# Sums of w_out from three pairs of buffers, four of the seven blocks by way of DRAM; weight blocks, x pieces and the first steps in another order

## The chip, the cores and the metric

One core of a Trainium2 chip runs the whole program. The metric is the device time of one execution in microseconds (us), the median of the runs shown. The engines are PE (TensorE, matrix products), DVE (VectorE), ACT (ScalarE), POOL (GpSimd) and SP (SyncE, which here issues the DMAs, in program order).

## The reference, cut to what matters

```python
def _attn_ref(q, k, v, g_norm):                  # q, k, v: 8 x 8 heads x 576 x 64
    kv = np.einsum('bhsd,bhse->bhde', k, v)
    out = np.einsum('bhsd,bhde->bhse', q, kv)
    rms = np.sqrt(np.mean(out * out, axis=-1, keepdims=True) + 1e-06)
    return (out / rms * g_norm).astype(np.float32)

def _moe_ref(x, w_in, w_out):                    # x: 4608 x 512, w_in: 512 x 2048, w_out: 2048 x 512
    h = x @ w_in
    g = h * np.cos(h)
    return (g @ w_out).astype(np.float32)

def _moe2_ref(x, w1, w2, w3, w_out):             # 512 -> 1024 -> 1024 -> 512
    h = (x @ w1) * (x @ w2) @ w3
    return (h @ w_out).astype(np.float32)

# reference: the attention's output as 4608 x 512 goes through _moe_ref, its result through _moe2_ref
```

## The kernel before, in words

**Three stages.** The attention and the product h = x @ w_in run together, in 144 steps; then g @ w_out in 63 parts; then the second MLP. A float32 operand of a product is split into a high and a low half (`split`: ACT copies the high half, DVE or POOL subtracts it for the low half), and a product is three passes of matmuls (`three`, L863 to L865).

**The steps.** Step n takes one block of 512 tokens and one of 16 column blocks of w_in: 12 matmuls of 128x512 into one of four PSUM banks (`emit_h`, emitted one step ahead). ACT takes the whole turns from h (r, L1392), DVE subtracts them (u, L1393), ACT takes the sine (L1366), and one step later DVE multiplies by h (u, L1367), which frees the bank: h of step n+4 waits for that product of step n. After each pair of column blocks POOL makes four differences of g (`form`, L828 to L831: tiles ta and tb), and SP stores u, ta and tb to DRAM tensors g, the seven right blocks of a seven-product scheme. Beside this run, placed by step numbers in `phases`: the attention of the later units of tokens (`plan_unit`: its squares, Newton steps for the norms on DVE, scaling `o` on POOL, L359), the pieces of x (`split_x`, high half ACT, low half DVE, L124), and the conversion of weight words to float32 (`plan_words`, `plan_w_in`: one ACT and four DVE operations per block, L152 to L160; w_out's blocks go to DRAM, tensors w_out). `first_steps` writes steps 0 to 7 by hand: its list `begins` says when a w_in block's conversion starts, `norms` computes the first units' norms on DVE, `rows` spreads them with matmuls on PE (L462), `scale` applies them, `split_x(1, c)` prepares the second x block.

**The left blocks.** From w_out, for each of four row pairs kk, come seven left blocks wl_l_kk: l = 0 and 1 are halves as they are, l = 2 is a half too, l = 3, 4, 5, 6 are sums and differences made one after the other in place. `left_load(kk)` loads the four pieces of w_out (256 KB each) into one pair of buffers of the `g` tag. `left_plain(kk)` (steps 124 to 136) splits l = 0 and 1. For the sums the pair is loaded again: kk = 0 at step 137 (`left_sums` at steps 139 to 141), kk = 1 at step 142, kk = 2 and 3 after the parts 1 and 3, with `left_sums` in parts 0 to 5 (lines L933 to L940 are its additions, on DVE, for kk = 2 and 3 two of four on POOL).

**The parts.** NS is 144; "NS+i" in the code is part i. Part i is 24 matmuls (L995) of a right block g_hl_i (1 MB, loaded by `load_right` four parts ahead as g_raw, split by `split_right` two parts ahead: ACT high, DVE or POOL low) with the left blocks l of its product, kk = 0 and 1 in the first half and 2 and 3 in the second. The order of products takes l = 0, 1, 4, 3, 5, 2, 6, two parts each; so the parts 0 to 3 need l = 0 and 1, the parts 4 and 5 l = 4, the parts 6 to 13 l = 3, 5, 2 and 6.

**What sets the order.** Through both stages the order of each engine's instructions is the program's, written out by hand; each engine, and SP's queue of DMAs, takes its instructions in that order, and an instruction that waits holds all behind it on its engine.

## Time and profile before

| what | value |
|---|---|
| median of the runs shown (3) | 1515.92 us (1515.26 to 1516.95) |
| the profiled execution | 1524.87 us, its span 1523.1 us |
| PE busy | 1462.8 us (96%) |
| DVE, ACT, POOL busy | 1011.2, 695.6, 598.7 us |
| mean granted clock of PE | 0.984 |
| moved by DMA | 295.60 MB, mean 194 GB/s |

The steps run from about 45 us to 553 us of the span, the parts from 553 us to about 910 us, and the second MLP after that. Busy times are unions of the instructions' times; PE's matmuls overlap in the records, so what a stretch of PE is worth is read from the number of its matmuls, not from its busy share. The clock column gives the share of full speed that PE was granted in a stretch.

### The profile page before, as it was taken

To read this page: it belongs to the slowest core of one execution; us is meant where nothing else is said; L and a number is where in the kernel's file an instruction comes from. 1 tells how busy PE (TensorE), PEld (TensorE's weight loads), DVE (VectorE), ACT (ScalarE), POOL (GpSimd) and SP (SyncE) were. 2 spreads that over 40 slices of the span, in tenths; PEclk is the share of its full clock that TensorE was granted. 3 is DMA by queue.
4 is the path that set the end of the run, shared out by engine and by line. 5 is a ranking of instruction groups with operands and counts; after the bars stand their busy time and mean duration, and the time that the engine had idled before them with its cause. 6 is when DMAs were issued, how large, how long until landed. Compare 5 with 4: busy or idle time off the path is not lost.

```text
span 1523.1 us, 21182 instructions
## 1 busy us (share of the span) xinstructions
PE 1462.8 (96%) x7632; PEld 1248.5 (82%) x7632; DVE 1011.2 (66%) x1489; ACT 695.6 (46%) x1320; POOL 598.7 (39%) x423
## 2 busy tenths in 40 slices
PE   8999999899989985999999998999999999999998
PEld 6777777676767864898888887999999988999997
DVE  3888876687686785899999337755544546545543
ACT  4556555445544544555555435434433334333331
POOL 0043862644464552212121326455444237344330
PEclk9999999999999997999999999999999999999999
DMA  8256986867765975999999765122102313233312
GB/s 317 98 181 216 304 255 187 281 206 262 246 223 185 353 262 189 338 356 358 365 365 352 254 206 180 42 77 76 70 29 83 112 62 110 75 101 124 125 63 77
DMA packets 143529, 295.60 MB, mean 194 GB/s; under 512 B 16096, under 2 KB 49984, under 8 KB 143424
## 3 DMA queue, kind: packets, MB, share of 16 engines
q1 hardware_dynamic: 142720, 293.66, 56.4%
q8 instruction: 60, 0.98, 0.3%
q10 hardware_dynamic: 704, 0.59, 0.1%
q14 instruction: 45, 0.37, 0.1%
HBM read 184.92 MB, written 109.27 MB: 193 GB/s over the span
## 4 chain that ended last, share of the span: by engine, by line
PE 80%; DVE 9%; DMA 4%; issue 3%; POOL 2%; ACT 1%; SPq 1%; ACTq 0%; POOLq 0%; DVEq 0%
PE X L1213 13%; PE X L995 12%; PE V L995 6%; PE V L1213 6%; PE h L863 6%; PE h L864 6%; PE h L865 6%; PE o L864 4%; PE o L863 4%; PE o L865 4%; PE Y L1213 3%; PE Y L995 3%; PE kv L272 2%; DVE x L124 2%; DVE u L1393 1%
## 5 line engine op out<-in xcount | busy, mean ns | idle before, releaser
L863 PE MATMUL h<-x,w_in 128*128 128x512 f32 x576 | 238.7, 414 | 11.8 <-DVE u L1367 11.8
L1213 PE MATMUL X<-xc,w 128*128 128x384 f32 x1152 | 226.2, 337 | 5.3 <-DVE wchl L124 3.1
L864 PE MATMUL h<-x,w_in 128*128 128x512 f32 x576 | 227.8, 395 | 1.6 <-DVE x L124 1.6
L865 PE MATMUL h<-x,w_in 128*128 128x512 f32 x576 | 227.1, 394 | 0.0
L124 POOL TENSOR_TENSOR xc<-x2r,xc 128x768 fp32r<-128x768 f32 x70 | 134.8, 1936 | 228.5 <-ACT xc L122 228.5
L995 PE MATMUL X<-g_hl,wl 128*128 128x512 f32 (+1 forms) x960 | 204.0, 372 | 17.9 <-ACT wl L122 13.3
L1213 PEld LDWEIGHTS X<-xc,w 128*128 128x128 f32 x1152 | 203.9, 188 | 13.0 <-DVE wchl L124 3.5
L995 PEld LDWEIGHTS X<-g_hl,wl 128*128 128x128 f32 x960 | 169.4, 191 | 49.9 <-ACT wl L122 14.1
L122 ACT ACTIVATE g_hl<-g_raw 128x1024 fp32r<-128x1024 f32 x126 | 126.3, 1051 | 101.3 <-PE V L995 34.9
L124 POOL TENSOR_TENSOR g_hl<-g_raw,g_hl 128x1024 fp32r<-128x1024 f32 x31 | 79.1, 2553 | 226.6 <-ACT g_hl L122 202.7
L1393 DVE SCALAR_TENSOR_TENSOR u<-h,r 128x512 f32<-128x512 f32 x136 | 93.3, 686 | 93.5 <-ACT r L1392 80.9
L863 PEld LDWEIGHTS h<-x,w_in 128*128 128x128 f32 x576 | 109.7, 190 | 44.6 <-DVE u L1367 15.6
L124 DVE TENSOR_TENSOR g_hl<-g_raw,g_hl 128x1024 fp32r<-128x1024 f32 x95 | 114.0, 1228 | 48.0 <-ACT g_hl L122 47.9
L1392 ACT ACTIVATE r<-h 128x512 int32<-128x512 f32 x136 | 81.0, 596 | 139.4 <-PE h L865 138.9
L1221 ACT ACTIVATE s<-X 128x384 f32<-128x384 f32 x144 | 66.7, 488 | 152.7 <-PE X L1213 152.6
L864 PEld LDWEIGHTS h<-x,w_in 128*128 128x128 f32 x576 | 109.9, 191 | 26.1 <-DVE x L124 4.0
L865 PEld LDWEIGHTS h<-x,w_in 128*128 128x128 f32 x576 | 109.6, 190 | 23.6
L1213 PE MATMUL V<-xc,w 128*128 128x384 f32 x576 | 116.2, 335 | 0.0
L863 PE MATMUL o<-wchl,ab 128*128 128x512 f32 x288 | 112.3, 391 | 0.7 <-DVE part L1304 0.6
L864 PE MATMUL o<-wchl,ab 128*128 128x512 f32 x288 | 113.0, 392 | 0.0
L865 PE MATMUL o<-wchl,ab 128*128 128x512 f32 x288 | 110.5, 393 | 0.0
L1366 ACT ACTIVATE u<-u 128x512 f32<-128x512 f32 x136 | 85.1, 626 | 51.3 <-DVE u L1393 51.3
(175 smaller groups left out, 2590.4 us busy)
## 6 DMA issues: line engine op xcount, KB each, us to landing
g_raw<-g SPq DMA_DIRECT2D x126, 512.0 KB
x2r<-x_all SPq DMA_DIRECT2D x44, 384.0 KB
kvraw<-in_kv_main_dram SPq DMA_DIRECT2D x32, 512.0 KB
g<-ta SPq DMA_DIRECT2D x32, 512.0 KB
g<-tb SPq DMA_DIRECT2D x32, 512.0 KB
g<-u SPq DMA_DIRECT2D x28, 512.0 KB
g<-u SPq DMA_DIRECT2D x40, 256.0 KB
part<-o SPq DMA_DIRECT2D x36, 256.0 KB
```

What stands on the lines that cost most here:

```text
L122: hi = nc.scalar.activation(dst[:, 0], src, AF.Copy)
L124: lo = lo_engine.tensor_tensor(dst[:, 1], src, f32(dst[:, 0]), ALU.subtract)
L272: nc.tensor.matmul(ps[d], k[:, d], v[:, d], start=fresh and i == 0, stop=i == NC, skip_group_check=True,)
L863: nc.tensor.matmul(ps, w[0], x[0], start=first, stop=False)
L864: nc.tensor.matmul(ps, w[0], x[1], start=False, stop=False)
L865: return nc.tensor.matmul(ps, w[1], x[0], start=False, stop=last).ins
L995: nc.tensor.matmul(ps, w[:, a, i2, ws], g[:, b, q], start=first and half == 0 and q == 0 and n == 0, stop=last and final and q == KH - 1 a ...
L1213: nc.tensor.matmul(ps, w[:, self.i, a, k], x[:, b, k], start=first and k == 0 and n == 0, stop=last and k == 1 and n == 2, skip_group_chec ...
L1221: copied.append(nc.scalar.activation(s, ps, AF.Copy).ins)
L1366: nc.scalar.activation(u, u, AF.Sin, bias=HALF_PI, scale=TWO_PI)
L1392: nc.scalar.activation(r, h_ps[n], AF.Identity, bias=0.25, scale=INV_2PI)
L1393: nc.vector.scalar_tensor_tensor(u, h_ps[n], INV_2PI, r, ALU.mult, ALU.subtract)
```

## The change

Five things change.

1. **First steps.** The conversion of the fourth w_in block of this stage starts at step 6 instead of step 3. `emit_h(6)` moves ahead of `rows(0)` and goes to the bank acc3; `emit_h(7)` moves ahead of `rows(2)`. `scale` and `split_x(1, c)` follow in another order.
2. **Units and weight words.** The last three units of the attention start at steps 78, 86, 93 instead of 77, 84, 91; eight of sixteen w_out blocks are converted at other steps.
3. **x pieces.** How many pieces go into a step is counted by their width, and in five ranges of steps (`LIGHT`) their low half is made on POOL instead of DVE.
4. **w_out's left blocks.** `left_load` uses three pairs of buffers (g0 and g1, wc0 and wc1, wc2 and wc3, and g0 and g1 again), each loaded once, at steps 117, 120, 121 and 127. `left_stage(kk, 0..3)` makes the sums at the steps 122+4kk to 125+4kk and splits l = 0, 1 and 4 at once; some additions go to POOL. `left_store` writes the sums for l = 3, 5 and 6 to DRAM (12 stores of 256 KB); l = 2 is read again from w_out. In the parts 0 to 7 `left_late` splits the four late blocks, two row pairs at a time, from a tile w_pair (512 KB) that `left_pair` loads two parts ahead.
5. **Loads ahead.** The first four `load_right` go to the steps 131, 135, 138 and 140 (before 126, 130, 134, 142), the first `split_right` to 138 (before 133); the conversion of the second MLP's weights starts in part 9 (before 8), its loads in part 7 (before 6).

```diff
@@ -582,7 +582,7 @@
         group = [begin()]
         emit_h(0)
         emit_h(1)
-        begins = (1, 1, 1, 1, 0, 0, 0, 0)
+        begins = (1, 1, 1, 0, 0, 0, 1, 0)
         for n in range(HM):
             attends = n < NPAIR
             new = []
@@ -590,8 +590,10 @@
                 rows(1)
             if n == 6:
                 rows(3)
-            if 1 <= n < HM - 1:
+            if 1 <= n < HM - 3:
                 emit_h(n + 1)
+            if n == 4:
+                emit_h(6, "acc3")
...
                 norms(sums, x, y, t)
                 rows(0)
             if n == 5:
+                emit_h(7)
                 scale(0)
                 rows(2)
+                split_x(1, 0)
             if n == 6:
                 scale(2)
-                split_x(1, 1)
-            if n == 7:
                 split_x(1, 2)
+                scale(3)
+                split_x(1, 3)
...
             if n == 5:
                 scale(1)
-                split_x(1, 0)
-            if n == 6:
-                scale(3)
+                split_x(1, 1)
...
-        split_x(1, 3)
         emit_h(HM)
 
     plan = {}
@@ -844,7 +845,7 @@
         at(n + lag, "top", store, 2, ta, tag_a)
         at(n + lag + (lag > 2), "top", store, 4, tb, tag_b)
 
-    def split_x(t, c, units=None):
+    def split_x(t, c, units=None, lows=None):
         if t not in x_hl:
             x_hl[t] = x_home(t % 3, [P, 2, KD, TB], F32R, f"x_{t}")
         done = 0
@@ -854,7 +855,7 @@
             if units is None or u in units:
                 made = split(
                     x_hl[t][:, :, c, done:done + w], o_sb[u][:, c, s:s + w],
-                    None if t == 0 else nc.vector,
+                    None if t == 0 else lows or nc.vector,
                 )
...
-    def emit_h(n):
+    def emit_h(n, tag=None):
         t, m = steps[n]
-        if n <= HM or n % 4 < 2:
+        if tag:
+            ps = ps_acc.tile([P, 512], F32, tag=tag, name=f"h_{n}")
+        elif n <= HM or n % 4 < 2:
             ps = ps_h.tile([P, 512], F32, tag="h", name=f"h_{n}")
         else:
             ps = ps_acc.tile([P, 512], F32, tag=f"acc{n % 4 - 2}", name=f"h_{n}")
@@ -892,19 +895,29 @@
 
     w_left = {}
 
-    def left_raw(kk, which):
-        t = g_home([P, 2, DM], F32, f"w_out_{which}{kk}")
-        for i in range(2):
-            nc.sync.dma_start(out=t[:, i], in_=later["w_out", 4 * kk + 2 * i + which])
-        return t
+    LEFT_TAGS = (("g0", "g1"), ("wc0", "wc1"), ("wc2", "wc3"), ("g0", "g1"))
+    sums_d = {}
+    lefts = {}
+
+    def left_load(kk):
+        f = []
+        for which, tag in enumerate(LEFT_TAGS[kk]):
+            name = f"w_out_{which}{kk}"
+            if tag[0] == "g":
+                t = g_home([P, 2, DM], F32, name, tag)
+            else:
+                t = homes["p2"].tile([P, 2, DM], F32, tag=tag, name=name)
+            for i in range(2):
+                nc.sync.dma_start(out=t[:, i], in_=later["w_out", 4 * kk + 2 * i + which])
+            f.append(t)
+        lefts[kk] = f
 
     def left_home(l, kk):
         if l == 0:
             return homes["p2"], f"wc{4 + kk}"
-        if l == 1:
-            return wpool, f"wi{kk}"
-        at = 4 + 5 * kk + (4, 3, 5, 2, 6).index(l)
-        return wpool, f"wi{at}" if at < NM else f"u{at - NM}"
+        if l in (2, 6):
+            return wpool, f"u{4 * (l == 6) + kk}"
+        return wpool, f"wi{4 * (1, 4, 3, 5).index(l) + kk}"
 
     def left(l, kk, src):
         pl, tag = left_home(l, kk)
@@ -912,34 +925,53 @@
         split(t, src, vec)
         w_left[l, kk] = t
 
-    lefts = {}
-
-    def left_load(kk):
-        lefts["at"] = left_raw(kk, 0), left_raw(kk, 1)
-
-    def left_plain(kk):
-        h = slice(0, DM // 2)
-        f0, f1 = lefts.pop("at")
-        left(0, kk, f0[:, :, h])
-        left(1, kk, f1[:, :, h])
-
-    def left_sums(kk, stage):
-        f0, f1 = lefts["at"]
+    def left_stage(kk, stage):
+        f0, f1 = lefts[kk]
         h = DM // 2
         a11, a21, a12, a22 = f0[:, :, 0:h], f0[:, :, h:], f1[:, :, 0:h], f1[:, :, h:]
-        adder = vec if kk < 2 else pool
         if stage == 0:
-            left(2, kk, a22)
-            vec.tensor_tensor(a22, a21, a22, ADD)
-            left(3, kk, a22)
+            (vec if kk < 2 else pool).tensor_tensor(a22, a21, a22, ADD)
+            left(0, kk, a11)
         if stage == 1:
-            adder.tensor_tensor(a21, a11, a21, SUB)
-            vec.tensor_tensor(a22, a22, a11, SUB)
-            left(4, kk, a22)
+            (pool if kk else vec).tensor_tensor(a21, a11, a21, SUB)
+            left(1, kk, a12)
         if stage == 2:
-            adder.tensor_tensor(a12, a12, a22, SUB)
-            left(5, kk, a21)
-            left(6, kk, a12)
+            vec.tensor_tensor(a11, a22, a11, SUB)
+        if stage == 3:
+            (pool if kk else vec).tensor_tensor(a12, a12, a11, SUB)
+            left(4, kk, a11)
+
+    def left_store(kk, l):
+        if l not in sums_d:
+            sums_d[l] = dram.tile([P, 4, 2, DM // 2], F32, name=f"w_left_{l}")
+        f0, f1 = lefts[kk]
+        h = DM // 2
+        src = {3: f1[:, :, h:], 5: f0[:, :, h:], 6: f1[:, :, 0:h]}[l]
+        nc.sync.dma_start(out=sums_d[l][:, kk], in_=src)
+
+    LATE_LEFT = [(l, q) for l in (3, 5, 2, 6) for q in range(2)]
+    pairs_l = {}
+
+    def left_pair(i):
+        if i >= len(LATE_LEFT):
+            return
+        l, q = LATE_LEFT[i]
+        t = g_home([P, 2, 2, DM // 2], F32, f"w_pair_{l}{q}")
+        if l == 2:
+            for k in range(2):
+                for e in range(2):
+                    c = 4 * (2 * q + k) + 2 * e + 1
+                    nc.sync.dma_start(out=t[:, k, e], in_=later["w_out", c][:, DM // 2:])
+        else:
+            nc.sync.dma_start(out=t, in_=sums_d[l][:, 2 * q:2 * q + 2])
+        pairs_l[i] = t
+
+    def left_late(i):
+        l, q = LATE_LEFT[i]
+        t = pairs_l.pop(i)
+        for k in range(2):
+            left(l, 2 * q + k, t[:, k])
+        left_pair(i + 2)
 
 
     parts_of = []
@@ -1313,9 +1345,10 @@
         }
         end_of = {t: max(n for n, s in enumerate(steps) if s[0] == t) for t in range(NB)}
         ready = plan_first(HM - 1)
-        starts = (14, 22, 29, 36, 44, 52, 59, 77, 84, 91)
+        starts = (14, 22, 29, 36, 44, 52, 59, 78, 86, 93)
         for u, n in zip(range(6, NU), starts):
             ready[u] = plan_unit(u, n, u in (6, 9, 10, 11, 12, 13))
+        LIGHT = (*range(48, 54), *range(64, 72), *range(80, 88), *range(98, 104), *range(114, 120))
         pieces = []
         for u in range(NHALF + 1, NU):
             for t in range(2, NB):
@@ -1324,37 +1357,37 @@
                     pieces.append((t, max(ready.get(u, 0), free) + 1, u))
         taken_up = {}
         for t, n, u in sorted(pieces):
+            w = min((t + 1) * TB, (u + 1) * HALF) - max(t * TB, u * HALF)
+            most = {4: 4, 5: 2}.get(u, 2 if t in (2, 3, 6) or u == 14 else 1.3) * HALF
             for c in range(KD):
-                while taken_up.get(n, 0) >= (4 if u == 4 else 2):
+                while taken_up.get(n, 0) + w > most:
                     n += 1
-                taken_up[n] = taken_up.get(n, 0) + 1
-                assert n < begin_of[t] - 1
-                at(n, "pieces", split_x, t, c, (u,))
+                taken_up[n] = taken_up.get(n, 0) + w
+                assert n < begin_of[t] - 1, (t, n, u, c)
+                at(n, "pieces", split_x, t, c, (u,), pool if n in LIGHT else vec)
         i = state["conv"]
         for k in range(i, n_first):
-            plan_w_in(k, (8, 9, 10, 12, 14, 16, 18, 20)[k - i])
-        words = (22, 36, 39, 52, 54, 67, 70, 73, 76, 79, 92, 95, 98, 101, 104, 107)
+            plan_w_in(k, (8, 9, 10, 12, 14, 16, 18)[k - i])
+        words = (22, 37, 39, 52, 54, 67, 69, 73, 75, 81, 93, 95, 99, 101, 105, 107)
         for k, n in enumerate(words):
             plan_words(n_first + k, n)
         for kk in range(4):
-            at(121 + 4 * kk, "top", left_load, kk)
-            at(124 + 4 * kk, "mid", left_plain, kk)
-        at(126, "end", load_right, 0)
-        at(130, "end", load_right, 1)
-        at(133, "mid", split_right, 0)
-        at(134, "end", load_right, 2)
-        at(137, "top", left_load, 0)
-        for k in range(3):
-            at(139 + k, "mid", left_sums, 0, k)
+            n = 122 + 4 * kk
+            at((117, 120, 121, 127)[kk], "end", left_load, kk)
+            for k in range(4):
+                at(n + k, "mid", left_stage, kk, k)
+            for l, k in ((3, 2), (5, 3), (6, 5)):
+                at(n + k, "top", left_store, kk, l)
+        at(131, "end", load_right, 0)
+        at(135, "end", load_right, 1)
+        at(138, "mid", split_right, 0)
+        at(138, "end", load_right, 2)
         at(140, "mid", split_right, 1)
-        at(142, "top", left_load, 1)
-        at(142, "end", load_right, 3)
-        for kk, n in ((1, 0), (2, 2), (3, 4)):
-            at(NS + n, "mid", left_sums, kk, 0)
-            at(NS + n, "mid", left_sums, kk, 1)
-            at(NS + n + 1, "mid", left_sums, kk, 2)
-            if kk < 3:
-                at(NS + n + 1, "end", left_load, kk + 1)
+        at(140, "end", load_right, 3)
+        at(NS - 2, "end", left_pair, 0)
+        at(NS - 1, "end", left_pair, 1)
+        for i in range(len(LATE_LEFT)):
+            at(NS + i, "mid", left_late, i)
 
         def do(n, where):
             for f in plan.pop((n, where), ()):
@@ -1413,10 +1446,10 @@
                 load_right(i + 4)
             if state["conv"] > state["put"]:
                 put(1)
-            if 8 <= i and state["conv"] < state["load"]:
+            if 9 <= i and state["conv"] < state["load"]:
                 convert(1)
-            if 6 <= i:
-                prefetch(min(state["conv"] + 2, len(chunks)))
+            if 7 <= i:
+                prefetch(min(state["conv"] + (1 if i == 7 else 2), len(chunks)))
             part(i)
             do(NS + i, "mid")
             do(NS + i, "end")
```

The order of instructions in three places; in the names, the last number counts tiles.

PE, first steps, before: h_5 ends, the first norms' rows (spread) follow, then h_6.

```order
L864 MATMUL h_5_673<-x_0_421,w_in_5_582 128x512
L865 MATMUL h_5_673<-x_0_421,w_in_5_582 128x512
L865 MATMUL h_5_673<-x_0_421,w_in5_582 128x512
L462 MATMUL spread_2_0_700<-rs_first_97 64x96 x6
L462 MATMUL spread_3_0_707<-rs_first_97 64x96 x6
L462 MATMUL spread_2_1_723<-rs_first_97 64x96 x6
L462 MATMUL spread_3_1_730<-rs_first_97 64x96 x6
L863 MATMUL h_6_737<-x_0_421,w_in6_627 128x512
```

PE at the same place, after.

```order
L866 MATMUL h_5_671<-x_0_421,w_in5_582 128x512
L864 MATMUL h_6_684<-x_0_421,w_in6_627 128x512
...
L866 MATMUL h_6_684<-x_0_421,w_in6_627 128x512
L462 MATMUL spread_2_0_711<-rs_first_97 64x96 x6
L462 MATMUL spread_3_0_718<-rs_first_97 64x96 x6
L462 MATMUL spread_2_1_727<-rs_first_97 64x96 x6
L462 MATMUL spread_3_1_734<-rs_first_97 64x96 x6
L864 MATMUL h_7_744<-x_0_421,w_in7_666 128x512
```

h_6 stands between h_5 and the first rows now; h_7 likewise stands ahead of the third row set.

DVE, parts 2 and 3, before: wl is a low half of a left block, w_out a sum in place, g_hl a low half of a right block.

```order
L124 TENSOR_TENSOR g_hl_4_5441<-g_raw_4_0_5345,g_hl_4_5441 128x1024
L124 TENSOR_TENSOR g_hl_4_5441<-g_raw_4_1_5347,g_hl_4_5441 128x1024
L124 TENSOR_TENSOR wl_2_2_5476<-w_out_12_5436,wl_2_2_5476 128x512
L933 TENSOR_TENSOR w_out_12_5436<-w_out_02_5433,w_out_12_5436 128x2x256
L124 TENSOR_TENSOR wl_3_2_5480<-w_out_12_5436,wl_3_2_5480 128x512
L937 TENSOR_TENSOR w_out_12_5436<-w_out_12_5436,w_out_02_5433 128x2x256
L124 TENSOR_TENSOR wl_4_2_5485<-w_out_12_5436,wl_4_2_5485 128x512
L124 TENSOR_TENSOR g_hl_5_5488<-g_raw_5_0_5394,g_hl_5_5488 128x1024
```

DVE at the same place, after: w_pair is the tile loaded from the stored sums, s1 a sum of results (it stood a few rows lower before).

```order
L124 TENSOR_TENSOR g_hl_4_5448<-g_raw_4_0_5361,g_hl_4_5448 128x1024
L124 TENSOR_TENSOR g_hl_4_5448<-g_raw_4_1_5363,g_hl_4_5448 128x1024
L124 TENSOR_TENSOR wl_5_0_5483<-w_pair_50_5397,wl_5_0_5483 128x512
L124 TENSOR_TENSOR wl_5_1_5486<-w_pair_50_5397,wl_5_1_5486 128x512
L124 TENSOR_TENSOR g_hl_5_5494<-g_raw_5_0_5406,g_hl_5_5494 128x1024
L1067 TENSOR_TENSOR s1_0_0_5422<-Y_0_0_2_5457,s1_0_0_5422 128x512
L1067 TENSOR_TENSOR s1_0_1_5436<-Y_0_1_2_5470,s1_0_1_5436 128x512
L124 TENSOR_TENSOR wl_5_2_5529<-w_pair_51_5444,wl_5_2_5529 128x512
L124 TENSOR_TENSOR wl_5_3_5532<-w_pair_51_5444,wl_5_3_5532 128x512
```

The sums in place (L933 and L937 here) are gone from the parts, and the splits that are left read w_pair.

SP, end of the steps, before: u, ta and tb are stores of g, g_raw and w_out loads.

```order
L961 DMA g_raw_4_0_5345<-g_0_0_950 128x1024
L961 DMA g_raw_4_1_5347<-g_0_1_1125 128x1024
L834 DMA g_4_3_5312<-u_7_7_5307 128x2x512
L835 DMA g_4_3_5312<-u_8_7_5092 128x512
L961 DMA g_raw_5_0_5394<-g_0_2_1592 128x1024
L961 DMA g_raw_5_1_5396<-g_0_3_1733 128x1024
L898 DMA w_out_02_5433<-w_out_8_3628 128x512
L898 DMA w_out_02_5433<-w_out_10_4162 128x512
L898 DMA w_out_12_5436<-w_out_9_3725 128x512
```

SP at the same place, after.

```order
L966 DMA w_pair_30_5335<-w_left_3_4831 128x1024
L835 DMA g_4_3_5328<-u_7_6_5267 128x2x512
L836 DMA g_4_3_5328<-u_8_6_5072 128x512
L966 DMA w_pair_31_5344<-w_left_3_4831 128x1024
L840 DMA g_4_3_5328<-ta_4_6_5329 128x2x512
L840 DMA g_4_3_5328<-tb_4_6_5330 128x2x512
L993 DMA g_raw_4_0_5361<-g_0_0_950 128x1024
L993 DMA g_raw_4_1_5363<-g_0_1_1125 128x1024
L966 DMA w_pair_50_5397<-w_left_5_4861 128x1024
```

The loads of w_out into the one pair of buffers are gone; the loads of w_pair stand between the stores of g and the loads of g_raw.

## Rows read from the trace of the kernel before

**Rows 1.** The page: one engine's busy us, share of the span, instructions.

```profile
PE 1462.8 (96%) x7632; PEld 1248.5 (82%) x7632; DVE 1011.2 (66%) x1489; ACT 695.6 (46%) x1320; POOL 598.7 (39%) x423
```

**Rows 2.** What PE waited for, whole span: us in total, times, longest us.

```profile
PE X L995 <- ACT wl L122: 13.3, 1, 13.3
PE h L863 <- DVE u L1367: 11.8, 7, 2.4
PE kv L272 <- DMA kvraw<-in_kv_main_dram: 8.4, 2, 4.5
PE Y L995 <- ACT g_hl L122: 4.6, 2, 3.9
PE X L995 <- ACT g_hl L122: 3.8, 1, 3.8
...
PE h L864 <- DVE x L124: 1.6, 6, 0.4
```

**Rows 3.** Windows: length, busy us (instructions) of five engines, clock, DMA share, GB/s.

```profile
325.00:350.00 25.00, 23.76 (x103) 18.67 (x101) 24.48 (x37) 11.82 (x25) 20.63 (x17) 1.00 0.82 271
...
425.00:450.00 25.00, 22.18 (x96) 17.69 (x96) 20.98 (x38) 11.12 (x24) 16.47 (x14) 1.00 0.54 174
450.00:475.00 25.00, 20.75 (x76) 16.22 (x76) 20.29 (x27) 9.25 (x19) 12.49 (x11) 0.86 0.78 290
...
550.00:575.00 25.00, 19.58 (x72) 14.86 (x71) 17.98 (x17) 9.64 (x14) 9.56 (x6) 0.86 1.02 388
575.00:600.00 25.00, 7.47 (x17) 5.14 (x18) 14.73 (x16) 9.94 (x13) 8.54 (x6) 0.60 0.52 171
600.00:625.00 25.00, 25.00 (x111) 20.64 (x110) 14.46 (x16) 12.38 (x16) 6.01 (x3) 0.99 0.74 241
```

**Rows 4.** The chain that ended last, 540 to 610 us: start, us, what.

```profile
566.24 5.66 DMA w_out<-w_out
...
579.41 2.46 POOL g_hl L124
...
585.32 4.56 DMA w_out<-w_out
...
589.96 0.64 ACT wl L122
```

**Rows 5.** Timeline of PE, first steps: start us, us, what, idle time before it.

```profile
66.97 3.34 PE L462 MATMUL spread<-rs_first 96*64 96x96 f32 x48 [1.82 <-DVE rs_first L327]
70.23 0.80 PE L863 MATMUL h<-x,w_in 128*128 128x512 f32 x1
...
75.23 2.20 PE L462 MATMUL spread<-rs_first 96*64 96x96 f32 x48
```

**Rows 6.** The chain that ended last, 290 to 300 us.

```profile
292.85 6.67 DMA kvraw<-in_kv_main_dram
```

**Rows 7.** Groups by shape, DVE, 330 to 360 us: busy us, mean ns.

```profile
L124 DVE TENSOR_TENSOR x<-o,x 128x288 fp32r<-128x288 f32 x4 | 2.4, 642 | 0.0
```

**Rows 8.** Tiles wl, w_out, 480 to 610 us: ns minimum/median/maximum, first, last start.

```profile
L124 DVE TENSOR_TENSOR wl<-w_out,wl x26: 680/693/1780, 500.2 to 603.9; 128x512 fp32r<-128x512 f32 x26
...
L936 POOL TENSOR_TENSOR w_out<-w_out x2: 1263/1268/1272, 574.2 to 592.2; 128x512 f32<-128x512 f32 x2
```

**Rows 9.** Timelines of DVE and, last line, POOL, 430 to 462 us.

```profile
433.49 1.78 DVE L157 SCALAR_TENSOR_TENSOR u_f<-u_w,u_f 128x512 int32<-128x512 int32 x1
...
436.89 0.68 DVE L1393 SCALAR_TENSOR_TENSOR u<-h,r 128x512 f32<-128x512 f32 x1
...
438.50 1.16 DVE L325 TENSOR_TENSOR rs<-rsx,rs 128x18 f32<-128x18 f32 x1
439.69 0.18 DVE L326 SCALAR_TENSOR_TENSOR rs<-rs,rs 128x18 f32<-128x18 f32 x1
...
447.59 1.29 POOL L828 TENSOR_TENSOR ta<-u,u 128x512 f32<-128x512 f32 x1 [7.97 <-DMA g<-ta]
```

**Rows 10.** A window over the last steps, columns as in rows 3.

```profile
500.00:540.00 40.00, 40.00 (x178) 33.13 (x177) 30.76 (x40) 21.63 (x36) 19.48 (x15) 1.00 0.83 308
```

## The prediction

> **What bounds the kernel now.** PE is busy 96% of the span [rows 1], so only its idle time and its slow stretches can be won. I read first the list of what PE waits for: the reader is to see one wait of 13.3 us for the high half of a left block (wl), two more of the parts' waits beside it (4.6 and 3.8 us for g_hl), seven waits of h for DVE's product u (11.8 us), and a wait for kvraw [rows 2]. Then the windows: where PE stands, its clock falls as well, so the loss is larger than the idle time [rows 3]. From 600 to 625 us PE runs 111 matmuls in 25.00 us, 0.225 us each; a step of 12 is then 2.70 us and a part of 24 is 5.40 us. From 550 to 600 us it ran 72 + 17 = 89, worth 20.0 us; 30.0 of the 50 us were lost, of which 50 - 19.58 - 7.47 = 22.9 as idle time, the rest to a clock of 0.86 and 0.60. Third, the chain of waits through that stretch says why [rows 4]: a load of w_out lands after 5.66 us, sums in place and POOL's queue (a g_hl of 2.46 us ahead of a sum) hold the pair of buffers, the next load is issued only then and takes 4.56 us, and the last splits follow at 589.96. It is a serial loop through one pair of buffers, once for each kk.
>
> From 425 to 475 us PE idles 2.82 + 4.25 = 7.1 us and loses some 0.14 x 20.75 = 2.9 us to the clock: 10 us [rows 3]. The seven waits of h for u make 11.8 us in all [rows 2]; the other 4.7 us lie between 336 and 356 us, where DVE is busy 24.48 of 25 us and POOL 20.63 [rows 3].
>
> **The first steps.** The first norms are waited for 1.82 us, and then h_6 runs from 70.23 to 75.23, 5.0 us in place of 2.7 [rows 5]: 1.8 + 2.3 = 4.1 us. The change puts h_6 ahead of those rows: PE then works through the wait, which was 1.82 us against h_6's 2.7, and need not fall to the lower clock. Of the six waits of h for x [rows 2] two lie just behind, worth 0.5 us. What is next late: the bank of h_9 needs the product of h_7 on DVE, whose scaling and x splits stand ahead of it. The moved w_in conversion (one ACT operation, four of DVE, and no DMA of its own) leaves steps 3 to 5 and lands in 6 and 7, where DVE has the scaling as well. I take **+3.5 us** of 4.6; between +1 (a new wait behind DVE takes most of it) and +4.5 (the two x waits as well).
>
> **Units, weight words, x pieces.** A wait for kvraw of about 4 us stands at 299.5: its load took 6.67 us and was issued only at 292.85, behind stores of the norms [rows 6]. Newton's steps ahead of it have one x piece less before them after the change; with the other waits for x (1.6 us in six [rows 2], less the 0.5 above) I take **+2 us**, between 0 (the load is late whatever the piece does) and +4 (all of one kvraw wait).
>
> For the 4.7 us at 336 to 356 us, DVE loses sixteen x pieces there to POOL. A piece of 128x288 costs DVE 0.64 us on the mean [rows 7], so counted by DVE's time alone this frees 10 us and all 4.7 would go. But the two engines hold each other up: a split of 128x512 on DVE takes 0.68 us at the least, 0.69 in the middle and 1.78 us at the most, a sum on POOL 1.26 [rows 8]; a small Newton operation of 0.18 us took 1.16 with POOL at work [rows 9]. POOL, 20.63 of 25 us busy there, gets the work, and the attention's scaling stands behind it on POOL. I take **+0.5 us**, between -2 and +4. The Trainium skill, SBUF — State Buffer, section "Who interferes with whom", says that DVE and GpSimd share one pair of SBUF ports under an exclusive lock, which a DVE operation with two SBUF inputs and a GpSimd operation that reads SBUF hold for the whole instruction, so that the other fully blocks. By that rule the pieces save nothing in a stretch where POOL is full (0 here), by DVE's busy time alone +4.7; the rows, 0.68 against 1.78, agree with the rule.
>
> At 436 to 466 us the same work stands: words u13 to u15, a unit's Newton steps and its x pieces. Newton moves two steps later, the words by one or two. Before, POOL stood still 7.97 us there, for a store that SP had queued late [rows 9], and in that gap Newton's later operations took 0.18 us; a conversion's operation with POOL at work took 1.78 [rows 9]. If POOL stays busy, eleven such operations cost up to 1 us more each, and the four of a conversion as much (1.78 less 0.69, the low end of rows 8). I take **-3 us**, between -7 (all of Newton contested, as priced) and +5 (half of the 10 us goes, since these pieces leave DVE).
>
> **The left blocks.** Gross, the 30.0 us go: nothing that the parts 0 to 5 need is made in them any more (l = 0, 1, 4 are split by step 137), and what is made late (l = 3, 5, 2, 6) is split six parts, 32 us, ahead of its matmuls. The 23 DVE and 4 POOL operations that the parts 0 to 5 carried become 16 splits spread over eight parts. Three things are to be paid.
>
> First, the steps 122 to 143. DVE did 17 such operations there (13 splits, 4 sums), now 20 (12 splits, 8 sums), twelve of them in the steps 122 to 129. Those steps last 8 x 2.70 = 21.6 us; DVE's two operations for each h are 0.68 us each [rows 9], 10.9 us in eight steps; the twelve cost between 12 x 0.69 = 8.3 and 12 x 1.78 = 21.4 us [rows 8]: 19 to 32 us. POOL gets eight sums of 1.26 us at the least [rows 8], 10 us, in steps 126 to 138, beside 19.48 us of work in the 40 us before them [rows 10]. The stretch had no wait of PE at all before: 40.00 of 40 [rows 10]. In the middle, DVE comes 4 us late, and a step's 2.7 us of it are covered by the four banks: **-2.5 us** with a wait for POOL's sum, between 0 and -8.
>
> Second, DMA. A part loads 1 MB of right block, now 0.5 MB of w_pair beside it: 1.57 MB in 5.40 us are 291 GB/s, and the last stores of g fall into the same time. The 550 to 575 us window moved 388 GB/s at a share of 1.02 [rows 3], with nothing left over, and PE's long wait after it (share 0.52) let the loads catch up. That cover is gone. Nearest rows: the two load times in the chain, 5.66 and 4.56 us [rows 4]; I take one of them, **-4.5 us**, in waits for g_hl in the parts 2 to 6, between 0 and -10.
>
> Third, the trip through DRAM: 12 stores of 256 KB and as many loads more on SP. Stores lie in the steps 124 to 139, the loads from step 142; the row for a load is 5.66 us, and two parts (10.8 us) lie between load and split. Hidden; if the stores hold SP, the stores of g behind them wait and with them POOL. **-1 us** for the rest, so the left blocks give 30 - 2.5 - 4.5 - 1 = **+22 us**, between 15 and 27. The loads moved in the steps (131 to 140) and the later conversion of the second MLP's weights have over 300 us until those are used: 0.
>
> **Sum.** 3.5 + 2 + 0.5 - 3 + 22 = 25 us. The profiled execution took 1524.87 us (span 1523.1), so after it 1500; the runs shown have a median of 1515.92, 0.6% shorter, and the waits are the same program's: 1515.9 - 25 = 1491.
>
> **Rivals.** *All stalls go*: DVE, relieved of the pieces, no longer makes h wait, and DMA keeps up. Gain 4.5 + 4 + 4.7 + 5 + 27 = 45: 1471. For it: DVE's busy time falls. Against: rows 8 and 9. Chance 0.17.
>
> *The stalls come back in the steps*: DVE and POOL contend in the steps 122 to 138 by the upper price (-8), DMA's refill costs 10, and the 436 us stretch loses 7: 3.5 + 2 + 0.5 - 7 + 30 - 8 - 10 - 1 = +10: 1506. For it: no spare DVE time by the upper price. Chance 0.2.
>
> *Slower*: the serial loop comes back in the parts. SP takes its queue in order: the load of w_pair for the next block waits until the split of the one before has freed its tile, and g_raw two parts ahead stands behind that load. A late w_pair then holds ACT, whose next g_hl stands behind its split, and PE waits for that g_hl. Each of the eight parts with such a split is then paced by two loads in series (w_pair, then g_raw, 5.66 us each by [rows 4]) and a split on ACT and DVE (0.64 [rows 4] + 0.69 [rows 8]), 12.7 us in place of 5.4: 8 x 7.3 = 58 us lost against 25 + 4.5 + 1 = 30.5 won otherwise: 1543. It decides from 5.4 + 30.5/8 = 9.2 us a part. Against it: two tiles and two parts of lead. Chance 0.06.
>
> *The wait only moves*: g_hl replaces wl at the same length because the loads are late anyway; the gain of 22 falls to nothing, the rest stays within 3 us: 1513 to 1519, half of it within 0.2%. Chance 0.05.
>
> **Numbers.** The forecast, 1484 to 1499, has 0.52. A difference of 0.2% (3 us) is about what a measurement of this kernel can tell from no change. The range reaches towards the first two rivals until no more than 0.2 is left out: 1470 to 1509. Faster 0.90, same 0.03, slower 0.07.
>
> **What would show it.** PE's wait for wl gone from the list, and 550 to 610 us without a stretch under 20 us of PE in 25; small waits for g_hl in parts 2 to 6 with a full DMA share (the second price); h_6 directly behind h_5 at full clock; waits of h for u still there at 336 to 356 and about 440 us, longer in the latter. Wrong would be: no waits of h for u left (contention overpriced), or new ones between 500 and 550 us over 8 us, or waits for g_hl over 10 us.

## The result, and the profile after

The changed kernel takes 1496.14 us (median of 4 runs, 1492.64 to 1498.46), the kernel before 1516.43 us beside it (1515.26 to 1518.55): a ratio of 0.9863, 95% interval 0.9839 to 0.9886, 20.3 us less. The forecast was 1491 us, in a range of 1470 to 1509.

The profiled execution of the changed kernel has a span of 1490.8 us (1492.64 us as a run), 32.3 us less than the one of before. That pair overstates the change: the profiled run of before lay 8.4 us above its median, the one of after 3.5 us below. What PE waited for now (us in total, times, longest), whole span:

```profile
PE h L864 <- DVE u L1400: 15.0, 8, 4.2
PE kv L272 <- DMA kvraw<-in_kv_main_dram: 6.5, 2, 5.1
PE X L1245 <- DVE wchl L124: 3.1, 1, 3.1
PE Y L1027 <- DVE g_hl L124: 2.7, 1, 2.7
PE h L864 <- DVE u_first L625: 2.1, 1, 2.1
PE Y L1027 <- POOL g_hl L124: 1.7, 1, 1.7
...
PE h L865 <- DVE x L124: 0.2, 1, 0.2
```

The wait for wl, 13.3 us in [rows 2], is gone, and so are the waits for ACT's g_hl (4.6 and 3.8). The waits of h for DVE's u are longer, 15.0 us in place of 11.8, with one of 4.2. Two waits for g_hl are left (2.7 and 1.7), and a new one for u_first (2.1). The windows, columns as in [rows 3]:

```profile
50.00:75.00 25.00, 23.70 (x194) 19.43 (x192) 21.66 (x55) 14.75 (x35) 0.00 (x0) 1.00 0.31 104
325.00:350.00 25.00, 23.09 (x93) 18.55 (x94) 18.50 (x29) 15.73 (x39) 19.93 (x26) 0.93 0.89 310
425.00:450.00 25.00, 17.92 (x69) 13.36 (x68) 24.52 (x37) 8.56 (x18) 16.55 (x15) 0.93 0.80 284
525.00:550.00 25.00, 22.14 (x89) 17.55 (x88) 13.98 (x14) 9.46 (x15) 19.09 (x14) 0.93 0.76 271
550.00:575.00 25.00, 23.27 (x93) 18.54 (x92) 18.94 (x18) 14.80 (x19) 7.57 (x4) 0.87 1.00 366
575.00:600.00 25.00, 25.00 (x112) 20.71 (x111) 22.34 (x24) 16.97 (x22) 5.80 (x3) 1.00 0.96 348
```

From 525 to 575 us, where the parts begin now, PE still stands short: 89 and 93 matmuls in place of 112, at a clock of 0.93 and 0.87. From 575 us on it is full. Against [rows 3], where 550 to 600 us held 72 + 17 matmuls, most of the hole is closed. Part of what is left is new: PE had run the last steps without a wait before [rows 10], and now it waits there too.

To see where the time went I take from PE's timeline the start of the first matmul of a step or a part. The stretches, in us, one profiled execution each:

| stretch | before | after |
|---|---|---|
| span's start to step 0 | 40.7 | 36.4 |
| step 0 to 24 (first steps) | 101.3 | 97.2 |
| step 24 to 66 | 143.3 | 142.0 |
| step 66 to 72 (the kvraw wait) | 25.7 | 21.6 |
| step 72 to 90 (336 to 356 us before) | 60.2 | 59.2 |
| step 90 to 120 (436 to 466 us before) | 101.5 | 101.5 |
| step 120 to 138 (the sums' steps) | 49.0 | 50.1 |
| step 138 to part 0 | 16.3 | 20.8 |
| part 0 to part 6 | 64.1 | 40.7 |
| part 6 to the end | 921.2 | 921.4 |

The parts began at 537.9 us before and begin at 528.8 us now; the 553 us named ahead of the prediction was misread. The first line is nobody's: no change touches it, and it lay between 35.0 and 42.2 us in twelve profiles. 23.4 us are won in the first six parts and 5.7 us lost in the steps from 120 on. Of the six parts five take 5.4 to 5.7 us now; part 3 alone takes 12.9 us. How most of this loss (the 4.5 us from step 138 on) and the long part 3 come about the chain of work shows (start, us, what), from 514 us on:

```profile
514.27 2.33 DVE g_hl L124
516.61 0.33 SPq L993
516.99 0.43 SPq L950
517.46 5.69 DMA g<-u
523.27 0.70 DVE u L1426
...
529.96 2.38 POOL g_hl L124
532.36 0.33 SPq L993
532.75 5.04 DMA g<-u
538.01 1.29 POOL ta L829
...
550.01 2.77 POOL g_hl L124
552.83 5.95 PE Y L1027 x17
```

SP takes its queue in order. The load of g_raw_2 stands at the end of step 138, and its buffers are free only when DVE has split g_hl_0 (its second half took 2.33 us beside POOL's ta and tb). Only then, at 516.99, SP issues the last store of a sum and at 517.46 the store of u; 5.69 us later that store has landed, and only then has DVE a place to write the next u. On DVE's timeline the same place is an idle time of 5.50 us, ended by a DMA of u to g:

```profile
517.11 0.67 DVE L1400 TENSOR_TENSOR u<-u,h 128x512 f32<-128x512 f32 x1
523.27 0.69 DVE L1426 SCALAR_TENSOR_TENSOR u<-h,r 128x512 f32<-128x512 f32 x1 [5.50 <-DMA g<-u]
```

PE's h waited 2.90 us for it at 521.7. The second half of the chain is the same once more: g_raw_3 waits for the split of g_hl_1 by POOL, the store of u behind it lands 5.04 us after its issue, POOL makes the next ta, which waited for that store, at 538.01 and g_hl_3 only at 550.01, for which PE waits in part 3. What SP itself waited for between 500 and 536 us:

```profile
SPq L993 <- DVE g_hl L124: 13.6, 3, 6.4
SPq L993 <- POOL g_hl L124: 5.6, 1, 5.6
```

### The profile page after: what moved, and what is told of

Read it like the earlier page. It is cut to its first block, busy times and chain, and to the rows that moved or that the text cites. A ratio compares the mean times of both kernels' runs of the same rounds, so it can differ in the third digit from the quotient of the medians.

```text
span 1490.8 us, 21208 instructions
## 1 busy us (share of the span) xinstructions
PE 1448.2 (97%) x7632; PEld 1239.4 (83%) x7632; DVE 1002.3 (67%) x1451; ACT 695.0 (47%) x1320; POOL 630.3 (42%) x461
## 4 chain that ended last, share of the span: by engine, by line
PE 80%; DVE 9%; DMA 5%; issue 3%; POOL 2%; ACT 1%; SPq 0%; POOLq 0%; DVEq 0%; ACTq 0%
PE X L1245 13%; PE X L1027 12%; PE V L1027 7%; PE V L1245 6%; PE h L864 6%; PE h L865 5%; PE h L866 5%; PE o L865 4%; PE o L864 4%; PE o L866 4%; PE Y L1245 3%; PE Y L1027 3%; PE kv L272 1%; DVE x L124 1%; DVE u L1426 1%
## 5 line engine op out<-in xcount | busy, mean ns | idle before, releaser
L864 PE MATMUL h<-x,w_in 128*128 128x512 f32 x576 | 237.9, 413 | 17.2 <-DVE u L1400 15.0
L1027 PE MATMUL X<-g_hl,wl 128*128 128x512 f32 (+1 forms) x960 | 200.2, 368 | 0.0
L124 DVE TENSOR_TENSOR g_hl<-g_raw,g_hl 128x1024 fp32r<-128x1024 f32 x95 | 117.1, 1259 | 44.1 <-ACT g_hl L122 43.9
```

What stands on the lines that cost most here:

```text
L124: lo = lo_engine.tensor_tensor(dst[:, 1], src, f32(dst[:, 0]), ALU.subtract)
L864: nc.tensor.matmul(ps, w[0], x[0], start=first, stop=False)
L1027: nc.tensor.matmul(ps, w[:, a, i2, ws], g[:, b, q], start=first and half == 0 and q == 0 and n == 0, stop=last and final and q == KH - 1 a ...
```

## The experiments

All ratios are to the kernel before, run beside the kernel in question, with 95% intervals; the changed kernel's is 0.9863 [0.9839, 0.9886].

**Left blocks and loads alone** (parts 4 and 5 of the change; the rest as before).

```diff
-        begins = (1, 1, 1, 0, 0, 0, 1, 0)
+        begins = (1, 1, 1, 1, 0, 0, 0, 0)
...
-        starts = (14, 22, 29, 36, 44, 52, 59, 78, 86, 93)
+        starts = (14, 22, 29, 36, 44, 52, 59, 77, 84, 91)
...
-                at(n, "pieces", split_x, t, c, (u,), pool if n in LIGHT else vec)
+                at(n, "pieces", split_x, t, c, (u,))
```

> The left blocks and the loads ahead alone (parts 4 and 5 of the change); first steps, units, weight words and x pieces as before. Theory: the parts 0 to 6 carry nearly all of the gain, +23 us there less 6 us in the steps 122 to 143: 1516 - 17 = 1499 us, with PE's wait for wl gone. Rival (the rest of the change carries over a third): 1504 us or more.

Measured 1499.96 us, 0.9884 [0.9866, 0.9902]: 18 of the 20 us. Parts 0 to 5 took 41.4 us in its profile, steps 138 to 143 took 20.6, and no wait for wl is left. The theory holds.

**First steps, undone and alone.** The changed kernel with the first steps as before, and the kernel before with the new first steps.

```diff
-        begins = (1, 1, 1, 0, 0, 0, 1, 0)
+        begins = (1, 1, 1, 1, 0, 0, 0, 0)
...
-            if n == 4:
-                emit_h(6, "acc3")
```

> The changed kernel with the first steps as before. Theory: the first steps' 3.5 to 4 us are lost again, 1499.5 to 1500 us, PE waits 1.8 us for the first norms and h_6 runs at the lower clock. Rival (the steps behind, bound by DVE, swallow it): 1496 us, with the stretch to step 30 ending at the same time after step 0 as in the changed kernel.

> The kernel before with the first steps of the change alone. Theory (forecast): 3.5 us less than before; from step 0 to step 24 97 to 98.5 us in place of 99.6 to 101.3. Rival (new waits behind the first steps take most of it back): under 1.5 us less, within what can be told from no change, with a wait of h for u_first near step 8 of 2 us.

Undone: 1496.72 us, 0.9863 [0.9842, 0.9883], no difference from the changed kernel. Alone: 1515.55 us (12 runs), 0.9988 [0.9972, 1.0004], 1.8 us. From step 0 to step 24 the profiles took 99.6, 99.6 and 101.3 us with the old first steps, and 97.2 in seven and 98.3 and 98.6 in two with the new ones: 2.4 us between the usual values. The waits are as named: with the new first steps alone PE's waits hold the u_first wait of 2.1 us, and wl's is still there.

```profile
PE X L998 <- ACT wl L122: 12.7, 1, 12.7
...
PE h L864 <- DVE u_first L625: 2.1, 1, 2.1
```

With the old first steps PE waits its 1.8 us for the first norms again, as the theory had it. The rival, by which the steps behind swallow the 2.4 us, does not hold: steps 24 to 66 took 142.5 us with the old first steps and 142.0 with the new ones. So the profiles show the gain, smaller than 3.5 us; it is of the size of the runs' scatter, and the medians, undone or alone, can't tell it from none.

**Units, words, x pieces undone.**

```diff
-        words = (22, 37, 39, 52, 54, 67, 69, 73, 75, 81, 93, 95, 99, 101, 105, 107)
+        words = (22, 36, 39, 52, 54, 67, 70, 73, 76, 79, 92, 95, 98, 101, 104, 107)
...
-                at(n, "pieces", split_x, t, c, (u,), pool if n in LIGHT else vec)
+                at(n, "pieces", split_x, t, c, (u,))
```

> The changed kernel with units, weight words and x pieces as before (parts 2 and 3 undone). Theory from the two traces, step 30 to 120: these parts give 1.6 + 4.0 + 1.0 + 0 = 6.6 us, so 1502 us, with a wait for kvraw of about 4 us back near step 66. Rival (the forecast's terms, +2 + 0.5 - 3): 1496 us. Rival (the other run's kvraw wait was chance): 1496 us with a short kvraw wait.

Measured 1497.04 us, 0.9873 [0.985, 0.9895]: the 6.6 us read from the two traces were wrong, the forecast's own small sum (2 + 0.5 - 3) is nearer. Steps 66 to 72 took 22.8 us here and 22.4 and 22.6 in the other two profiles with the old pieces: the 25.7 of before were that one execution's. With the new pieces these steps took 21.0 to 22.4 us in seven profiles (24.4 in the mixture below). Steps 72 to 90 took 59.9 against 59.2 with the change, steps 90 to 120 took 99.2 against 101.5.

**All x pieces on DVE**, in the steps of the change.

```diff
-                at(n, "pieces", split_x, t, c, (u,), pool if n in LIGHT else vec)
+                at(n, "pieces", split_x, t, c, (u,), vec)
```

> The changed kernel with every x piece's low half on DVE, in the same steps; nothing else moved. Theory (DVE and POOL hold each other up, so that the engine that takes a piece matters little): steps 66 to 120 within 2 us of the changed kernel's, 1496 us. Rival (DVE's own busy time counts): the 36 pieces of some 0.6 us that come back to DVE, 20 us, make h wait longer, 5 us or more, 1501 us and above.

Measured 1500.55 us, 0.9891 [0.9866, 0.9916]. Steps 72 to 90 took 63.2 us in place of 59.2, steps 90 to 120 101.9 in place of 101.5. The window from 325 to 350 us, columns as above:

```profile
325.00:350.00 25.00, 20.04 (x73) 15.95 (x74) 24.42 (x43) 13.07 (x35) 11.42 (x10) 0.86 0.91 305
```

DVE is busy 24.42 us of 25 there and PE runs 73 matmuls; with the pieces on POOL it was 18.50 us and 93. My theory falls at the first place and holds at the second: where DVE has nothing to spare, a piece given to POOL did help, by 4.0 us, near the rival's 5. (34 pieces change their engine, not 36.) A likely reason is on the timelines of the changed kernel: DVE's two operations for each h do not lengthen beside POOL, 0.68 and 0.67 us at 516.50 and 517.11 while POOL's tb ran from 515.46 to 517.74, and 0.69 and 0.68 on the mean of all 136.

**Third and fourth right block loaded later.** Nothing else moves; first both, then the third alone.

```diff
-        at(138, "end", load_right, 2)
+        at(139, "end", load_right, 2)
...
-        at(140, "end", load_right, 3)
+        at(142, "end", load_right, 3)
```

> The changed kernel with the third and fourth load_right at the end of step 139 and 142 in place of 138 and 140. Theory: the wait of 2.9 us at step 141 and most of the 4.4 us of waits in the parts 3 and 4 come from SP's queue, where g_raw_2 and g_raw_3 wait for the splits of g_hl_0 and g_hl_1 and hold the stores of u and ta behind them; then the 2.9 us and its slow clock go and 1490 to 1492 us remain. Rival (DVE late from the sums and contention): the 2.9 us stay, 1496 us. Rival (DMA refill): the 2.9 us go, the waits in the parts grow by as much, 1495 us.

> The changed kernel with only the third load_right moved, from the end of step 138 to that of 139; the fourth stays at 140. Theory (SP's wait for g_hl_0 holds the store of u ahead of step 141, its wait for g_hl_1 the later ones): the wait of 2.9 us at step 141 goes, step 138 to part 0 takes 16.3 us in place of 20.8, and the waits in the parts 3 and 4 stay: 1490 to 1492 us. Rival (the fourth load alone matters): 20 us there and 1496 us.

Both: 1486.22 us, 0.9785 [0.9767, 0.9803], 10 us under the changed kernel, more than the theory had. The third alone: 1491.90 us, 0.9844 [0.9816, 0.9872]. By the ratios the gain of both is 12 us, of one 3. In both profiles steps 138 to 143 took 16.3 us again, as before the change; with both loads early they took 19.7 to 22.4 in five profiles. The first six parts took 37.2 us with both and 39.0 with one, and 38.2 to 42.3 in those five. PE's waits with both:

```profile
PE h L864 <- DVE u L1400: 12.1, 7, 4.2
...
PE Y L1027 <- POOL g_hl L124: 2.2, 1, 2.2
```

The 2.9 us of h for u are gone (12.1 in seven waits), and one wait for g_hl on POOL remains.

**Late left blocks one part later, then two right halves on DVE as well.** The first is made on top of the kernel with both loads later, the second on top of the first.

```diff
-            at(NS + i, "mid", left_late, i)
+            at(NS + 1 + i, "mid", left_late, i)
```

> The kernel of the later loads with the late left blocks split one part later (parts 1 to 8 in place of 0 to 7). Theory (a late w_pair holds ACT and DVE, and the split of g_hl_3 stands behind it, as the forecast's third rival has it in its mechanism): the 2.3 us that PE still waits in part 3 and the slow clock behind it go: 3 to 4 us less than the kernel of the later loads, 1482 to 1483 us. Rival (g_hl_3's second low half waits for POOL's ta and tb alone): no change, 1486 us. Rival (the blocks come too late then): a new wait for wl in the parts 6 to 13, 1488 us or more.

Measured 1485.11 us, 0.9788 [0.9761, 0.9814]: no change; the wait of 2.1 us is still there. On POOL's timeline the split of g_hl_3 follows ta and tb without a gap, so the rival was right:

```profile
540.13 1.74 POOL L831 TENSOR_TENSOR tb<-u 128x512 f32<-128x512 f32 x1
541.82 1.30 POOL L832 TENSOR_TENSOR tb<-u,ta 128x512 f32<-128x512 f32 x1
543.08 2.35 POOL L124 TENSOR_TENSOR g_hl<-g_raw,g_hl 128x1024 fp32r<-128x1024 f32 x1
```

```diff
-            split(..., pool if r and i % 2 else vec)
+            split(..., pool if r and i % 2 and i > 3 else vec)
```

> The kernel of the later loads and later splits, with the second low half of g_hl_1 and g_hl_3 on DVE in place of POOL. Theory (the wait left in part 3 is POOL's: g_hl_3 stands behind ta and tb there, and DMA's refill costs nothing): the 2.1 us wait and the slow clock behind it go, the parts 0 to 5 take 32.7 to 33.5 us in place of 36.7, 1481 to 1482 us. Rival (the right blocks' loads themselves are late, DMA being full): a wait of g_hl for ACT or DMA of 2 us or more takes its place, 1485 us.

Measured 1481.88 us, 0.9783 [0.9757, 0.9809]. By the ratio this can't be told from the two kernels ahead of it (0.9785 and 0.9788); what shows the gain is the profile. Part 3 was the long part in every other kernel with the new left blocks: 10.8 to 14.0 us with both loads early, 11.6 with one later, 9.5 to 10.0 with both later, and 5.44 here. The first six parts took 32.64 us, 5.44 each, and PE waits for nothing in them (windows, then its waits over the whole span):

```profile
525.00:550.00 25.00, 25.00 (x112) 20.70 (x111) 19.85 (x18) 12.40 (x17) 17.52 (x11) 1.00 0.99 369
550.00:575.00 25.00, 25.00 (x112) 20.71 (x111) 18.37 (x20) 17.28 (x23) 6.70 (x3) 1.00 1.03 389
```

```profile
PE h L864 <- DVE u L1400: 12.2, 7, 4.2
PE kv L272 <- DMA kvraw<-in_kv_main_dram: 7.5, 3, 4.9
PE X L1245 <- DVE wchl L124: 3.1, 1, 3.1
PE h L864 <- DVE u_first L625: 2.1, 1, 2.1
```

The DMA share is 0.99 and 1.03 in these windows and PE full: the refill that I had priced at 4.5 us costs PE nothing, and no row of the list is a g_hl any more.

**A mixture for the steps 90 to 120**: the later loads, with the last units, and the words after step 75, as before and no piece on POOL after step 87.

```diff
-        starts = (14, 22, 29, 36, 44, 52, 59, 78, 86, 93)
+        starts = (14, 22, 29, 36, 44, 52, 59, 77, 84, 91)
...
-        LIGHT = (*range(48, 54), *range(64, 72), *range(80, 88), *range(98, 104), *range(114, 120))
+        LIGHT = (*range(48, 54), *range(64, 72), *range(80, 88))
```

> The kernel of the later loads with the last three units, the weight words after step 75 as before, and no x piece on POOL after step 87. Theory (by the traces, the steps 90 to 120 take 101.5 us with the change and 99.2 us without it, because POOL is kept busy beside Newton's steps and a conversion): 2.3 us less, 1484 us, and the steps 66 to 90 as in the changed kernel, 80 to 81 us. Rival (the two differ by chance of the clock): 1486 us.

Measured 1489.69 us, 0.9816 [0.9789, 0.9843]. Steps 90 to 120 took 102.6 us, not 99.2, and steps 66 to 72 24.4: a miss. The 99.2 us are of two kernels with the new left blocks and the old pieces; the kernel before and the first steps alone have the old pieces too and took 101.5 and 101.9 us. That difference lies in steps 115 and 116, 9.2 and 9.3 us against 11.7 and 11.6: with the old left blocks POOL's next ta there stands still 7.97 [rows 9] and 7.87 us until an earlier ta's store has landed, with the new ones 6.33 and 6.34 us until a conversion on DVE ends. The mixture has the new left blocks and is not slow there (9.9 us); it lost its time in steps 109 to 112 (17.2 us against 14.5); why, no run takes apart.

## Why the prediction held, and where its steps failed

**First steps (+3.5).** The step was right in kind. h_6 and h_7 fill the wait for the norms; the first spread has no idle time before it now, where [rows 5] had 1.82 us, and takes 2.20 us in place of 3.34:

```profile
63.48 2.20 PE L462 MATMUL spread<-rs_first 96*64 96x96 f32 x48
```

The clock of the window from 50 to 75 us is 1.00. The next late thing is the one that was named, h_9's bank, with 2.1 us. The term was some 1 to 2 us too large: 2.4 us by the usual profiles, 1.8 us (-0.6 to 4.2) by the run of this part alone.

**Units, words, x pieces (+2, +0.5, -3).** Their sum, about 0, is what undoing them showed (0.001 of the time, within the intervals), but not for the reasons given. Of the kvraw wait about 1 us went (steps 66 to 72, 22.4 to 22.8 us with the old pieces, 21.6 with the new), where I had +2. For the steps 72 to 90 I argued that POOL's help would be taken back by contention and took +0.5; the result, +0.7 to +1.0, is two larger effects that nearly cancel: the new places of units, words and pieces cost 3.3 us (59.9 to 63.2, with all pieces on DVE), and POOL gives 4.0 back. The failed step is the contention argument: the Trainium skill's rule (SBUF — State Buffer, "Who interferes with whom"), by which a GpSimd operation that reads SBUF holds up a DVE operation with two SBUF inputs for its whole length, I had read as if it made the choice of engine worth 0. The 4.0 us decide against the sum that I made of the rule, though the rows below still show what it describes. The 4.2 us wait that is left in these steps is Newton's on DVE with POOL at work, in the chain from 317 us (start, us, what):

```profile
317.73 1.17 DVE rs L325
318.92 1.23 DVE rs L326
320.17 1.22 DVE rs L327
321.41 1.22 DVE rs L325
322.66 0.19 DVE rs L326
```

Four operations take 1.2 us each and one 0.19; before, it was 1.16 against 0.18 [rows 9]. For the steps 90 to 120 I had -3. Against the two kernels that have the new left blocks with the old pieces it is -2.3, and the mechanism is the one named: from 428 us on four of Newton's operations take 1.06 to 1.22 us beside POOL's ta and tb, where one did before [rows 9]. Against the profile of before the stretch shows 0, because the left blocks gave 2.3 us in steps 115 and 116, which the forecast did not have; the waits of h there are 7.1 us in all before and after, the longest 2.4 and now 3.6.

**Left blocks (+22).** The hole was 30.0 us by [rows 3]; over the full pace of 5.44 us a part (32.6 us for six) it was 31.4 us in the profile of before and 28.8 in that of the first steps alone. It went, as worked out, and 18 us, the 2.3 us of steps 115 and 116 among them, arrived. Of the payments, one was near its size, one was not due, one was not measured by itself (the trip through DRAM, -1), and the one priced at nothing failed:

- The sums in the steps (-2.5): steps 120 to 138 lost 1.2 us, and 0.9 to 1.2 in every kernel with them. About half of the price.
- DMA's refill (-4.5): 0. The window was full, as forecast, and the sign named for this price appeared, waits for g_hl of 2.7 and 1.7 us in part 3. But they came of the order of loads and splits: the kernel with the later loads, the later splits and the two right halves on DVE runs its parts at full pace under a share of 0.99 to 1.03.
- **The loads moved in the steps (0)**: this is the step that failed. I priced them by when their data is used, with 300 us to spare; that holds for the second MLP's weights, but the third right block is loaded from 514.4 us and used from 540.0. Their price is what stands behind them in SP's queue: a load that waits for its buffer holds stores, and DVE and POOL wait for the places that those stores free. By the profiles it cost 4.5 us in the steps 138 to 143 and 3.5 us in the parts (1 to 5 by the scatter of part 3); moving two loads by one and two steps gave back 10 us in the medians. The first split of a right block goes from step 133 to 138 in the change, and the third load cannot start before it, but stands there.

I had charged 8 us in all; 13.8 were lost, 5.7 in the steps from 120 on and 8.1 over full pace in six parts. The profiles, one of each kernel, divide them: 1.2 for the sums, 8.0 for the two loads, and 4.6 that are left, of which 4.1 are the two right halves on POOL behind ta and tb, taken away by the choice of engine (36.7 to 32.6); 0.5 lie between the two kernels ahead of it (37.2 and 36.7), within the scatter. The third rival had the mechanism, SP's order, but placed it at w_pair and priced it as if nothing overlapped; w_pair's later split changed nothing.

**The time.** 25 us were forecast and 20.3 measured. The left blocks alone gave 18 in place of 22: the price of the loads and of the halves on POOL was not counted, the refill's was charged and not due, the sums' was half of what was charged, and 2.3 us came in steps 115 and 116. That these errors offset each other in part is luck; the path that was to be won, the loop through one pair of buffers, was read rightly.

## What to carry to other kernels

Price a moved load by the queue it waits in, not only by when its data is needed: a load whose buffer is not free stops every store behind it, and each store may free a place that another engine waits for. When a long stall is taken out, look in the new trace for the first engine that waits for the store of a tile it has to reuse, and place the loads behind the stores there. A forecast that rests on one profile should be scaled to the median of the runs, since waits and clock in one execution can be 8 us off.

## What was not expected of the hardware

- The time from the start to step 0 was 35.0 to 42.2 us in twelve profiles of kernels that do the same up to there.
- The same wait of 2.1 us at step 9 left the clock of the window from 75 to 100 us at 1.00 in the changed kernel and at 0.93 in the kernel with the old x pieces and in the kernel with two right halves on DVE. These two are the profiles in which steps 0 to 24 took 98.6 and 98.3 us in place of 97.2.
- DMA shares of 0.99 to 1.03 at 369 and 389 GB/s for 50 us cost PE nothing, once the order of loads and splits was right.
